# RWKV attention with a squared-ReLU feed-forward layer on one core: state products inside the mixing step, one pool of four PSUM banks, a re-calibrated planner with new order tables

## The chip, the cores and the metric

The kernel runs on one core of a Trainium2 chip, as one program. The metric is device time in microseconds, median of three runs. TensorE (PE) multiplies matrices into PSUM, of which the kernel uses eight banks of 128 partitions x 512 fp32; VectorE (DVE), ScalarE (ACT) and GpSimd (POOL) compute element-wise; SyncE (SP) issues nearly all transfers. Each engine works through its instructions in program order, and semaphores order the engines among each other.

## What is computed

```python
# r, k, v, w: (4, 8, 768, 48); u: (8, 48); w_in: (384, 2048); w_out: (2048, 384)
for t in range(S):
    kt, vt, rt, wt = (k[:, :, t], v[:, :, t], r[:, :, t], w[:, :, t])
    cur = np.einsum('bhd,bhe->bhde', u[None] * kt, vt)
    y[:, :, t] = np.einsum('bhd,bhde->bhe', rt, state + cur)
    state = wt[:, :, :, None] * state + np.einsum('bhd,bhe->bhde', kt, vt)
x = y.transpose(0, 2, 1, 3).reshape(B * S, H * D)
h = np.maximum(x @ w_in, 0.0)
return (h * h) @ w_out
```

The recurrence has 768 steps, four batches and eight heads of 48; its output is 3072 rows of 384 for the feed-forward layer.

## The kernel before

The sequence is cut into six chunks (c = 0 to 5) of 128 tokens. An attention unit is one chunk of one batch (24 units); heads lie in four pairs, each pair on 112 partitions. Inside a chunk the recurrence becomes matrix products: w is accumulated by a scan, and r and k are scaled by the products of w.

The steps of a unit, with their lines: transfers of w, k, r (L449 in chunk 0, L455 later) and v (L486); in chunk 0 three `turn` steps on TensorE (L502) that bring the inputs into the transposed layout by fp32 products with a permutation, later a DVE transpose (L464) and sixteen small transfers (L474); the scan (L514), logarithm and exponential (L521, L522), the scalings (L525, L548 to L551); `beta`, the sums for u (TensorE in chunk 0, L538; POOL and DVE later); the diagonal from beta (L561); the scores `mt` (L572, sixteen fp32 matmuls in the profile, into two banks); the causal mask (L576); `ktp` and `kt`, the transposed k (L584, L586); the mixing step `mix`, which adds state times r (`inter`, L604, 48-row weights) and scores times v (`part`, L612, 128-row weights); its split into a high and a low part (`x`, L644 and L645); and the state products `dS` (`outer`, L664, 128-row weights, v times k) that DVE and POOL add to the state (L670 to L673). A TensorE step of products on small fp32 tiles has a `mode` other than 0 in the plan; here "a visit" is a stretch of such steps with only other work (feed-forward products and transposes) before and after it.

The feed-forward layer runs over 16 column blocks f per chunk, for all four batches at once (128 x 512) or, in chunks 0 (f below 6) and 1, for two batches at a time (128 x 256): the first product `hp` (L693, nine matmuls), ReLU on ACT (L698), squaring on DVE or, in chunk 0, ACT (L702, L700), the split in a high and a low part (L704, L705), and the second product `ob` (L711, three matmuls for each batch). Weights come in eight groups (L396, L398; 1.57 MB a group) and are turned into a high and a low fp32r part (L409 to L430).

PSUM: four banks are the accumulators `ob`, two the pool `hp` of the first product, two the pool `a` of all attention steps. A score step or a mixing step from chunk 1 on needs two banks of `a` at once.

What sets the order: every step goes to `Plan.add` with an engine, an estimated cost, a rank, what it reads and writes, and the pool slots it needs. `Plan.order` simulates the engines with these costs and always takes the step that can start first, ties by rank; the steps are then emitted in that order, so the program's order is fixed when it is built. Ranks come from the tables in `Ranks` (L196 to L221). TensorE steps pay 0.094 us when the mode changes. Where the plan sees TensorE idle before 110 us it puts in transposes of the identity as fillers (L755), ten at the start. At the very end the overflow flag is made (L750 to L754) and read by all engines (L762).

## Time and profile before

| | |
|---|---|
| median of three runs | 545.43 us (544.31 to 545.88) |
| profiled execution, its own time | 546.6 us |
| its span, first to last instruction | 544.8 us |
| mean granted TensorE clock | 0.993 |
| TensorE busy | 532.6 us (98%), 4243 matmuls |
| VectorE, ScalarE, GpSimd busy | 351.4, 300.3, 94.5 us |
| first `turn` matmul, first feed-forward matmul | 5.77 us, 43.91 us |
| read from and written to HBM | 31.66 MB, 4.72 MB |

How to read it: times in the trace count from the first instruction. A row of the timeline gives start, length, engine, line, operation, output <- inputs, shapes and count; neighbouring matmuls of one line are merged, and the length runs to the end of the last, so the next row can start before it. Therefore costs are read from start to start. In a table by stretches each row has the stretch, its length, the busy time and count of PE, PEld (weight loads), DVE, ACT and POOL, then the granted TensorE clock, the share of the DMA engines and GB/s. A group row has the total busy time, the mean of one in ns, and the idle time before with what ended it. An fp32 matmul stands twice in the profile.

### The profile page before, as it was taken

How to read it: one execution, taken by the hardware profiler on the slowest of the kernel's cores; microseconds unless marked ns; L12 is line 12 of the kernel's file. 1: busy time of each engine (PE TensorE's matmuls, PEld its weight loads, DVE VectorE, ACT ScalarE, POOL GpSimd, SP SyncE). 2: the span in 40 equal slices, each digit the busy share in tenths (PEclk: the TensorE clock that was granted, in tenths of full speed). 3: DMA queues.
4: the chain of work that ended last, by engine and by line, in shares of the span. 5: the costliest groups of instructions: out<-in, count | busy, mean ns of one | idle time of the engine just before them, and what ended most of it. 6: DMA issues, size and time to landing. Idle time of an engine off the chain costs nothing.

```text
span 544.8 us, 11043 instructions
## 1 busy us (share of the span) xinstructions
PE 532.6 (98%) x4243; PEld 472.8 (87%) x4243; DVE 351.4 (65%) x653; ACT 300.3 (55%) x728; POOL 94.5 (17%) x111
## 2 busy tenths in 40 slices
PE   7999999999999999999999999999999999999994
PEld 7978998889998989888888888889888998999894
DVE  4899788989795959596685684948443333333331
ACT  2877989886756675583834377464332232333221
POOL 2046543634030301212030030200000000000000
PEclk9899999999999999999999999999999999999998
DMA  8998893665946576774668155770011000000001
GB/s 212 268 228 174 189 260 83 134 128 79 182 80 109 119 87 123 84 157 59 84 121 111 29 104 101 122 96 1 0 45 45 0 1 0 31 31 0 1 0 62
DMA packets 195913, 50.92 MB, mean 93 GB/s; under 512 B 184080, under 2 KB 190736, under 8 KB 195856
## 3 DMA queue, kind: packets, MB, share of 16 engines
q1 hardware_dynamic: 195536, 49.77, 47.3%
q8 instruction: 35, 0.57, 0.5%
q10 hardware_dynamic: 320, 0.40, 0.2%
q14 instruction: 22, 0.18, 0.1%
HBM read 31.66 MB, written 4.72 MB: 67 GB/s over the span
## 4 chain that ended last, share of the span: by engine, by line
PE 81%; SPq 6%; DMA 5%; DVE 5%; ACT 1%; issue 1%; DVEq 0%
PE hp L693 34%; PE ob L711 34%; SPq L474 4%; PE a L612 3%; DMA ri<-in_moe_w_in_dram 3%; PE a L572 3%; PE a L604 2%; PE a L664 2%; DMA pt<-st 1%; SPq L449 1%; DVE st L464 1%; PE a L584 1%; SPq L455 1%; SPq L486 1%; DVE pt L551 1%
## 5 line engine op out<-in xcount | busy, mean ns | idle before, releaser
L711 PE MATMUL ob<-wo,g 128*128 128x384 f32 x1152 | 227.0, 341 | 0.0
L693 PE MATMUL hp<-x,wi 128*128 128x512 f32 (+1 forms) x1062 | 222.7, 355 | 0.0
L711 PEld LDWEIGHTS ob<-wo,g 128*128 128x128 f32 x1152 | 200.1, 188 | 10.3 <-issue 2.6
L693 PEld LDWEIGHTS hp<-x,wi 128*128 128x128 f32 x1062 | 174.1, 188 | 26.2 <-issue 0.9
L698 ACT ACTIVATE t<-hp 128x512 f32<-128x512 f32 (+1 forms) x118 | 61.0, 517 | 120.6 <-PE hp L693 106.3
L702 DVE SCALAR_TENSOR_TENSOR hp<-hp,t 128x512 f32<-128x512 f32 (+1 forms) x96 | 58.2, 606 | 89.7 <-ACT t L698 89.3
L705 DVE TENSOR_TENSOR g<-hp,g 128x512 fp32r<-128x512 f32 (+1 forms) x118 | 69.0, 585 | 37.8 <-ACT g L704 37.0
L704 ACT CAST g<-hp 128x512 fp32r<-128x512 f32 (+1 forms) x118 | 59.6, 505 | 53.8 <-DVE hp L702 53.4
L561 ACT ACTIVATE m<-ident,beta 128x128 f32<-128x128 f32 x192 | 60.6, 398 | 1.2 <-DVE beta L546 1.1
L576 DVE COPY_PREDICATED m<-caus,a 128x512 f32<-128x512 uint8 x48 | 34.1, 733 | 6.4 <-PE a L572 5.0
L645 DVE SCALAR_TENSOR_TENSOR x<-a,x 112x128 fp32r<-112x128 f32 (+2 forms) x64 | 20.6, 345 | 24.1 <-ACT x L644 22.6
L514 DVE TENSOR_TENSOR_SCAN pt<-pt,zero 112x128 f32<-112x128 f32 x80 | 30.0, 422 | 5.7 <-DMA pt<-st 5.5
L644 ACT ACTIVATE x<-a 112x128 fp32r<-112x128 f32 (+2 forms) x64 | 18.5, 322 | 21.1 <-PE a L612 8.5
L572 PEld LDWEIGHTS a<-pt 48*128 48x128 f32 x384 | 23.9, 187 | 6.5 <-issue 3.2
L572 PE MATMUL a<-pt 48*128 48x128 f32 x384 | 28.7, 285 | 0.6 <-DVE pt L551 0.6
L612 PE MATMUL a<-m,v 128*48 128x128 f32 (+1 forms) x384 | 26.9, 279 | 0.4 <-DVE m L576 0.2
L543 POOL TENSOR_TENSOR st<-st 128x384 f32<-128x384 f32 x20 | 20.9, 1049 | 36.9 <-DVE st L464 27.9
L464 DVE STREAM_TRANSPOSE st<-st 128x1152 f32<-128x1152 f32 x20 | 26.4, 1352 | 0.5 <-DMA st<-in_r_dram 0.5
L530 POOL COPY Ec<-pt 112x4 f32<-112x4 f32 x20 | 7.4, 372 | 102.7 <-DVE pt L514 101.7
L612 PEld LDWEIGHTS a<-m,v 128*48 128x48 f32 (+1 forms) x384 | 19.9, 128 | 5.7 <-issue 4.2
L430 POOL TENSOR_TENSOR wi<-q,wi 128x768 fp32r<-128x768 f32 x8 | 16.8, 2100 | 29.4 <-ACT wi L429 23.1
L545 POOL TENSOR_TENSOR st<-st,un 128x384 f32<-128x384 f32 x20 | 21.4, 1072 | 1.3
(96 smaller groups left out, 432.9 us busy)
## 6 DMA issues: line engine op xcount, KB each, us to landing
pt<-st SPq DMA_DIRECT2D x80, 96.0 KB, 3.1
ro<-in_moe_w_out_dram SPq DMA_DIRECT2D x8, 768.0 KB, 6.8
v<-in_v_dram SPq DMA_DIRECT2D x24, 192.0 KB, 4.1
st<-in_w_dram SPq DMA_DIRECT2D x10, 384.0 KB, 3.7
st<-in_k_dram SPq DMA_DIRECT2D x10, 384.0 KB, 5.2
st<-in_r_dram SPq DMA_DIRECT2D x10, 384.0 KB, 5.3
pt<-st SPq DMA_DIRECT2D x80, 48.0 KB, 3.6
out_dram<-q SPq DMA_DIRECT2D x20, 192.0 KB, 2.5
```

What stands on the lines that cost most here:

```text
L464: V.transpose(out=zt[:, i].rearrange("a t p q i -> a t (p q) i"), in_=sv[:, :, i].rearrange("s t p q x -> s t (p q) x"))
L514: lambda p=p: V.tensor_tensor_scan(out=pt[:, 0, p], data0=src(0)[:, p], data1=zero.broadcast_to([HP, C]), initial=1.0, op0=ALU.mult, op1=A ...
L561: A.activation(mv(j)[:, p], ident, AF.Copy, scale=beta.tile[:, 2 * p + j:2 * p + j + 1])
L572: T.matmul(mts[j].tile.rearrange("s (p t) -> s p t", p=NP)[:, p], pt[js, 2, p], pt[js, 1, p], start=True, stop=True)
L576: lambda j=j: V.copy_predicated(out=mv(j), mask=caus.unsqueeze(1).broadcast_to([128, NP, C]), data=mts[j].tile.rearrange("s (p t) -> s p t ...
L612: T.matmul(spot(p)[to:to + n + D], vt.tile[:, o - n:o + D], mv(j)[:, p], start=(c == 0 and p == SPLIT), stop=True, skip_group_check=True)
L693: T.matmul(hp.tile[:, 0:n], wi[f][:, wl, kt], xT[:, kt, xl, xs], start=(m == 0), stop=(m == 3 * KT - 1))
L698: P.add("act", 0.5 if full else 0.28, rank("g"), lambda: A.activation(t(), h(), AF.Relu), r=[hp], w=[(g, 1)])
L702: P.add("dve", 0.61 if full else 0.33, rank("g"), lambda: V.scalar_tensor_tensor(out=h(), in0=h(), scalar=0.0, in1=t(), op0=ALU.max, op1=A ...
L704: P.add("act", 0.53 if full else 0.31, rank("g"), lambda: A.copy(out=hi(), in_=h()), r=[hp], w=[(g, 0)])
L705: P.add("dve", 0.61 if full else 0.33, rank("g"), lambda: V.tensor_tensor(out=lo(), in0=h(), in1=hi().bitcast(F32), op=ALU.subtract), r=[h ...
L711: T.matmul(obs[b][:, 0:DM], g.tile[0][:, gl, o:o + C], wo[f][:, wl], start=(f == 0 and m == 0), stop=(f == NF - 1 and m == 2))
```

## The change

- The state products move from a step of their own (`dS`) into the mixing step of chunks 1 to 4: `mix` now runs `outer`, `inter`, `part`. Their results lie in the free columns of the bank `far_yb`, so no further bank is taken. Chunk 0 keeps its `dS` step; chunk 5 has no state.
- `hp` and `a` become one pool of four banks, which the first feed-forward product shares with all attention steps.
- The planner: engines begin at given times, a transfer has its own issue cost, costs are adjusted, entering small tiles costs 0.095, leaving them 0.28, a change between two small shapes 0.1, and an engine may wait up to 0.02 to 0.055 us for a step of better rank. Before 7.8 us TensorE steps count 1.9 times. `KEEP`, which made small-tile steps stay together, becomes a large negative number.
- All order tables are new, and a table `F` moves single steps.
- The transposed u is made after the first `turn`, the flag's matmul gets an early rank, and the tile `gap` (16 columns) moves the addresses of what follows.

```diff
-    SWITCH, KEEP = 0.094, 1.0
+    BEGIN = {"sp": 0.8, "pe": 3.75, "dve": 3.0, "pool": 3.4, "act": 2.1}
+    ENTER, LEAVE, SWAP, KEEP = 0.095, 0.28, 0.1, -1189.25
+    HOLD = {"pe": 0.042, "act": 0.055, "dve": 0.0264}
+    COLD, filler, WARM = 7.8, None, 10
...
-                    if pick is None or (t, order) < (at, first_order):
-                        at, pick, first_order = t, s, order
+                    can.append((t, order, s))
+                if can:
+                    limit = min(x[0] for x in can) + self.HOLD.get(unit, 0.0)
+                    at, _, pick = min((x for x in can if x[0] <= limit), key=lambda x: x[1])
...
-                bank = next((x[1] for p in ("a", "hp") for x in self.pools.get(p, ()) if x[0] <= idle), None)
+                bank = next((x[1] for x in self.pools["a"] if x[0] <= idle), None)
...
-                        free[unit] += self.SWITCH
+                        free[unit] += self.SWAP if mode and s.mode else self.ENTER if s.mode else self.LEAVE
...
-    OFF = {'hp': 1, 'g': -172, 'ob': 6.25, 'os': -416.25}
+    OFF = {'hp': 1063.5, 'g': -7297.25, 'ob': 9685.5, 'os': 2989.25}
...
-    P.pool("hp", hps)
-    P.pool("a", pas)
+    P.pool("a", pas + hps)
...
+        dS = far_yb if c else Slot("a")
+        dv = lambda: dS.tile[0:HP, NP * C - NP * J:].rearrange("a (p e) -> a p e", p=NP)[:, :, 0:D]
...
             def mix():
+                if not last:
+                    outer()
                 inter()
                 part((*TILES, SPLIT))()
...
-            mixed = P.add("pe", 1.45, rank("mix"), mix, r=[vt, *Ms, ("S", b), *RK], w=[yb, far_yb], mode=3, claim=[x3])
+            P.add("pe", 1.44 if last else 1.88, rank("mix"), mix, r=[vt, *Ms, ("S", b), *RK, *(() if last else (Kt,))], w=[yb, far_yb], mode=3, claim=[x3])
...
-            P.add("pe", 0.5, rank("dS"), outer, r=[vt, Kt], w=[dS], mode=3, after=[mixed] if c else [])
+            if c == 0:
+                P.add("pe", 0.443, rank("dS"), outer, r=[vt, Kt], w=[dS], mode=3)
...
-        hp, g = Slot("hp"), Slot("g")
+        hp, g = Slot("a"), Slot("g")
```

What the order makes of it on TensorE around the state of one pair of batches, before (`a_148` and `a_149` are the attention banks, `ob` the accumulators, L664 the state products of two units, L711 and L693 feed-forward):

```order
L711 MATMUL ob_144<-wo_67,g_98 128x384 x3
L711 MATMUL ob_145<-wo_67,g_98 128x384 x3
L664 MATMUL a_148<-v_154,m_159 64x48
L664 MATMUL a_148<-v_154,m_159 48x48
...
L664 MATMUL a_149<-v_155,m_163 64x48
L664 MATMUL a_149<-v_155,m_163 48x48
...
L711 MATMUL ob_144<-wo_67,g_100 128x384 x3
L693 MATMUL hp_146<-x_134,wi_73 128x256 x9
```

and in the changed kernel around a pair of mixing steps (L660 the state products, L653 `inter`, L668 `part`, L618 scores, L743 the first feed-forward product):

```order
L618 MATMUL a_149<-pt_131 128x128
L660 MATMUL a_150<-v_156,m_162 64x48
...
L653 MATMUL hp_148<-pt_131,S_134 64x128
...
L668 MATMUL hp_148<-m_161,v_156 64x128
...
L660 MATMUL a_149<-v_157,m_164 64x48
...
L653 MATMUL hp_147<-pt_131,S_135 64x128
...
L668 MATMUL hp_147<-m_160,v_157 64x128
...
L743 MATMUL hp_148<-x_136,wi_65 128x256 x9
L743 MATMUL a_150<-x_136,wi_69 128x256 x9
```

The state products no longer stand between feed-forward steps; scores and two mixing steps follow one another, they take all four banks, and the first feed-forward products come straight behind them in the same banks. In the whole program the visits go from 61 to 41: from 49 to 28 in chunks 1 to 5, and from 12 to 13 in chunk 0.

The beginning of SP's queue before (`st` are inputs of chunk 0, `ri` and `ro` raw weights):

```order
L449 DMA st_136<-in_w_dram 128x1x384
L449 DMA st_136<-in_k_dram 128x1x384
L449 DMA st_136<-in_r_dram 128x1x384
...
L486 DMA v_91<-in_v_dram 128x8x48
L449 DMA st_137<-in_w_dram 128x1x384
...
L396 DMA ri_56<-in_moe_w_in_dram 112x512 x2
```

and now:

```order
L439 DMA ri_68<-in_moe_w_in_dram 112x512 x2
L439 DMA ri_68<-in_moe_w_in_dram 48x512 x2
L439 DMA ri_68<-in_moe_w_in_dram 16x2x512 x2
L441 DMA ro_70<-in_moe_w_out_dram 128x2x768
L492 DMA st_138<-in_w_dram 128x1x384
L492 DMA st_138<-in_k_dram 128x1x384
```

A whole weight group (group 3) now stands ahead of the first inputs of chunk 0.

The beginning of TensorE's queue before (L755 are fillers, L363 the transposed u):

```order
L755 MATMUL a_148<-ident 128x128 x10
L363 MATMUL hp_146<-ident,m_158 112x8
L502 MATMUL ob_142<-perm,st_136 64x64
L502 MATMUL ob_142<-perm,st_136 48x64
L502 MATMUL ob_142<-perm,st_136 64x64
```

and now:

```order
L805 MATMUL a_149<-ident 128x128 x58
L545 MATMUL ob_143<-perm,st_138 64x64
L545 MATMUL ob_143<-perm,st_138 48x64
L545 MATMUL ob_143<-perm,st_138 64x64
L545 MATMUL ob_143<-perm,st_138 48x64
```

There are 58 fillers ahead of the first turn, and none anywhere later; before there were ten, and 64 more between the steps of chunk 0.

More of the change, by code (lines that the diff above doesn't have):

```diff
@@ L55, in pool, with add @@
         self.pools[name] = [[0.0, t] for t in tiles]
-    def add(self, engine, cost, rank, fn, r=(), w=(), after=(), runs=128, port=False, mode=0, claim=()):
+    def add(self, engine, cost, rank, fn, r=(), w=(), after=(), runs=128, port=False, mode=0, claim=(), issue=0.64):
         s = Step()
@@ L361 @@
         nc.scalar.dma_start(out=u8[:, j * J:j * J + D], in_=u)
-    us = Slot("hp")
-    P.add("pe", 0.1, -300, lambda: T.transpose(out=us.tile[0:HP, 0:H], in_=u8, identity=ident[0:H, 0:H]), w=[us])
+    us = Slot("a")
     def columns():
@@ L395, in load_w @@
             n = 2 * PC if i > KT else to.shape[0]
-            P.add("sp", 0.4 if i > KT else 0.0059 * n, rank, lambda to=to, src=src: nc.sync.dma_start(out=to, in_=src),
-                  w=[("wi", g, i)], after=before, runs=n)
+            P.add("sp", 0.3 if i > KT else 0.0066 * n, rank, lambda to=to, src=src: nc.sync.dma_start(out=to, in_=src),
+                  w=[("wi", g, i)], after=before, runs=n, issue=0.46)
         P.add("sp", 2.4, rank, lambda: nc.sync.dma_start(out=wo_r[g], in_=w_out32[g]), w=[("wo", g, 0, 0)],
-              after=before, runs=256)
+              after=before, runs=256, issue=0.41)
     def split_w(g, rank):
@@ L502, in turn @@
                             T.matmul(to[j * J:j * J + n, :, :, y], rows[:, y * D:y * D + n], pick[:, :, j], start=True, stop=True, skip_group_check=True)
-                P.add("pe", 1.0, rank("turn"), turn, r=[(st, ui, i)], w=[ps[i]], mode=3)
+                turned = P.add("pe", 0.94, rank("turn"), turn, r=[(st, ui, i)], w=[ps[i]], mode=3)
+                if b == 0 and i == 0:
+                    P.add("pe", 0.1, rank("turn"), lambda: T.transpose(out=us.tile[0:HP, 0:H], in_=u8, identity=ident[0:H, 0:H]), w=[us], after=[turned])
+                    P.add("act", 0.3, rank("turn"), columns, r=[us], w=["ut"])
             def tl(x):
@@ L604, in inter, with outer @@
                     T.matmul(spot(p)[to:to + n + D], Ss[b][js, PC + p * D - n:PC + p * D + D], pt[js, 1, p],
[L605 removed]
+                             start=(p == 0 or p == 3 and last), stop=False, skip_group_check=True)
+        def outer():
+            for p in range(NP):
+                for j in range(2):
+                    o, n = vo(2 * p + j), (J, D)[j]
+                    T.matmul(dv()[j * J:j * J + n, p], kv(Kt)[:, p, j * J:j * J + n], vt.tile[:, o:o + D],
+                             start=(p == 0), stop=True, skip_group_check=True)
         def part(ps):
@@ L695, in ffn @@
         full = n == 512
-        P.add("pe", 2.09 if full else 1.07, rank("hp"), first, r=wkeys("wi") + [x for b in range(*bs) for x in xkeys(c, b)], w=[hp])
+        P.add("pe", 2.085 if full else 1.067, rank("hp"), first, r=wkeys("wi") + [x for b in range(*bs) for x in xkeys(c, b)], w=[hp])
         hi, lo, t, h = (lambda: g.tile[0][:, 0, 0:n]), (lambda: g.tile[0][:, 1, 0:n]), (lambda: g.tile[1][:, 0:n]), (lambda: hp.tile[:, 0:n])
```

97 lines of the change are left out of this document (47 added, 50 removed), and 33 rows, old and new, of the table F.

## The prediction

> **What bounds the kernel now.** I began with the page's head and its chain of waits.
>
> ```profile
> span 544.8 us, 11043 instructions
> ...
> PE 532.6 (98%) x4243; PEld 472.8 (87%) x4243; DVE 351.4 (65%) x653; ACT 300.3 (55%) x728; POOL 94.5 (17%) x111
> ...
> GB/s 212 268 228 174 189 260 83 134 128 79 182 80 109 119 87 123 84 157 59 84 121 111 29 104 101 122 96 1 0 45 45 0 1 0 31 31 0 1 0 62
> ...
> PE 81%; SPq 6%; DMA 5%; DVE 5%; ACT 1%; issue 1%; DVEq 0%
> ```
>
> TensorE is busy for 98% of the span and 81% of the chain. The profiled execution took 546.6 us for a span of 544.8, 1.2 above the median of 545.43 of the three timed runs. I work out a difference on the span and take it from that median. A measurement of this kernel can tell about 0.3% (1.6 us) from no change.
>
> Next, the table by stretches of time:
>
> ```profile
> 20.00:40.00 20.00, 19.71 (x280) 17.15 (x277) 18.97 (x33) 15.74 (x39) 5.47 (x5) 0.96 1.01 238
> 100.00:120.00 20.00, 20.00 (x176) 16.97 (x175) 17.34 (x29) 18.44 (x46) 9.44 (x9) 1.00 0.63 100
> 500.00:520.00 20.00, 20.00 (x102) 18.10 (x101) 6.59 (x10) 5.38 (x10) 0.00 (x0) 1.00 0.00 1
> ```
>
> The second number is TensorE: 20.00 of 20.00 in the later rows, and no other engine is as full. So after the first 45 us a change gains only by taking work, or the dead time between matmuls, from TensorE. In the first 45 us the transfers are full too (DMA share 1.01), and TensorE's busy time there contains fill-in transposes. So I priced two things apart: the visits to attention work in the steady part, and the start.
>
> **A visit and its price.** The timeline around three visits of the state products (L664), and an undisturbed stretch:
>
> ```profile
> 145.90 2.88 PE L711 MATMUL ob<-wo,g 128*128 128x384 f32 x15
> 148.70 0.67 PE L664 MATMUL a<-v,m 128*64 128x48 f32 x16
> 149.30 0.79 PE L711 MATMUL ob<-wo,g 128*128 128x384 f32 x3
> 149.93 1.23 PE L693 MATMUL hp<-x,wi 128*128 128x256 f32 x9
> 151.09 0.67 PE L664 MATMUL a<-v,m 128*64 128x48 f32 x16
> ...
> 234.07 1.13 PE L664 MATMUL a<-v,m 128*64 128x48 f32 x32
> 235.13 2.38 PE L693 MATMUL hp<-x,wi 128*128 128x512 f32 x9
> ...
> 447.13 2.27 PE L711 MATMUL ob<-wo,g 128*128 128x384 f32 x12
> 449.24 2.26 PE L693 MATMUL hp<-x,wi 128*128 128x512 f32 x9
> 451.34 2.27 PE L711 MATMUL ob<-wo,g 128*128 128x384 f32 x12
> ```
>
> I go from start to start. Undisturbed, twelve L711 take 2.11 (0.53 for three) and nine L693 of 512 columns 2.10 (1.05 for nine of 256). Sixteen L664 alone take 149.30 - 148.70 = 0.60; thirty-two in one visit take 1.06. So a step costs 0.46 in work and 0.14 to finish; the three L711 after it take 0.63 (0.10 more), the nine L693 ahead of the next visit 1.16 (0.11 more). One visit to small fp32 tiles costs 0.14 + 0.10 + 0.11 = 0.35 beyond its work.
>
> **The change, term by term.**
>
> *Visits.* The instruction order has 61 stretches of such work between other work before and 41 now: in chunks 1 to 5, 49 become 28 (nine were state products by themselves, the rest are score and mixing steps that now stand side by side), and chunk 0 has 13 for 12. 20 x 0.35 = -7.0 (bounds 0.33 to 0.38 each). The products themselves stay, 0.46 a step.
>
> *Changes of shape inside.* Each of 16 merged steps goes from 128-row products to 48-row ones, which a separate step did at its edge; four more score steps now stand directly against other attention work. The nearest rows:
>
> ```profile
> 311.93 0.67 PE L604 MATMUL a<-pt,S 48*64 48x128 f32 x16
> 312.53 1.09 PE L612 MATMUL a<-m,v 128*64 128x128 f32 x16
> ```
>
> Sixteen L604 up to the change to 128 rows take 0.60, where sixteen matmuls of the state step take 0.46: at most 0.14 for a change, at least 0. I take 0.1: 16 x 0.1 = +1.6 and 4 x 0.1 = +0.4. The Trainium skill speaks against the merger here: its page "TensorEngine Tiling (Array Packing)", section Key Properties, says that changing the tiling mode drains TensorE. By it the merger would keep the drain and only move it; the sum with the full price stands below as a rival.
>
> *A later start.* Now the rows of the start:
>
> ```profile
> 0.81 0.70 SPq L449 DMA_DIRECT2D st<-in_w_dram  x1
> ...
> st<-in_w_dram SPq DMA_DIRECT2D x4, 192.0 KB, 3.8
> ...
> 18.00:20.00 2.00, 2.00 (x44) 2.00 (x44) 1.37 (x3) 2.00 (x7) 0.00 (x0) 0.52 1.14 294
> ```
>
> ```profile
> 1.60 2.39 PE L755 MATMUL a<-ident 128*128 128x128 f32 x10 [1.60 <-POOL ident masks.py:199]
> ...
> 5.77 6.42 PE L502 MATMUL ob<-perm,st 128*64 128x64 f32 x128
> 12.12 1.05 PE L538 MATMUL ob<-ut,pt 112*128 112x2 f32 x8
> 13.11 2.08 PE L502 MATMUL hp<-perm,st 128*64 128x64 f32 x64
> ...
> 26.89 2.73 PE L755 MATMUL a<-ident 128*128 128x128 f32 x23
> 29.56 1.57 PE L572 MATMUL a<-pt 48*128 48x128 f32 x16
> 31.05 1.86 PE L755 MATMUL hp<-ident 128*128 128x128 f32 x15
> ...
> 43.91 2.26 PE L693 MATMUL hp<-x,wi 128*128 128x256 f32 x17
> ```
>
> SP's first seven issues now fetch weight group 3, 1.57 MB, ahead of the first attention input. At 212 GB/s (first slice of the page) to 294 (18 to 20 us) these take 5.3 to 7.4 us; with issue at 0.81 and 3.8 to land, the first turn starts at 9.9 to 12.0. TensorE meanwhile does 58 transposes from 1.60 on: at the first ten's rate (2.39 for ten) till 15.5, at the rate of 26.89 to 29.56 (2.67 for 23) till 8.3. With some twenty slow ones it is 1.6 + 20 x 0.24 + 38 x 0.116 = 10.8. I take 10.5, against 5.77: +4.7 (bounds +4.1 to +9.7).
>
> *Faster first turns.* 128 turn matmuls took 12.12 - 5.77 = 6.35, while 64 later took 1.87 (2.08 less the last one's 0.2), so 3.74 for 128: the first ran at half rate. After 58 transposes they should run at full rate: -2.6 (bound: 0).
>
> *Waits of chunk 0.* The fill-in transposes show how long TensorE waited there:
>
> ```profile
> L755 PE MATMUL a<-ident 128*128 128x128 f32 x46 | 6.8, 309 | 1.6 <-POOL ident masks.py:199 1.6
> L755 PE MATMUL hp<-ident 128*128 128x128 f32 x28 | 4.3, 281 | 0.0
> ```
>
> 6.8 + 4.3 less the first ten's 2.4 is 8.7 us of waiting. The new order has two score steps ahead of the first feed-forward product (43.91 here) instead of three, and takes batch 1 right through to its state before batch 0. The chains from scan to mask that TensorE waits for stay as long, and the pauses are no longer filled. I take -1.0: one score step's work of about 1 us moves out of the way. On SP the values (v) of batch 2 now stand behind 11.6 MB: five weight groups, twelve inputs and five other v. At 236 GB/s (mean of the page's first three slices) they land near 50 us, about when their mixing step is due; a TensorE wait of up to 3 us there is the upper bound. Bounds -4 and +3.
>
> *Tail.*
>
> ```profile
> 537.31 0.19 PE L753 MATMUL a<-one,flag 128*1 128x1 f32 x2
> 537.54 0.15 DVE L754 TENSOR_SCALAR flag_i<-a 1x1 int32<-1x1 f32 x1 [3.71 <-PE a L753]
> 537.61 0.91 DVE L719 COPY m<-ob 128x384 f32<-128x384 f32 x2
> ```
>
> The last copies stand behind the flag; it goes early now: -0.2.
>
> *Shared banks.* What empties a bank, of feed-forward (L698, L702) and of the mixing step (L645):
>
> ```profile
> L698 ACT ACTIVATE t<-hp 128x512 f32<-128x512 f32 (+1 forms) x118 | 61.0, 517 | 120.6 <-PE hp L693 106.3
> L702 DVE SCALAR_TENSOR_TENSOR hp<-hp,t 128x512 f32<-128x512 f32 (+1 forms) x96 | 58.2, 606 | 89.7 <-ACT t L698 89.3
> L645 DVE SCALAR_TENSOR_TENSOR x<-a,x 112x128 fp32r<-112x128 f32 (+2 forms) x64 | 20.6, 345 | 24.1 <-ACT x L644 22.6
> ```
>
> Before, feed-forward had two banks to itself; ACT then waited for TensorE 106.3 us in all, so those banks were ready in time. Now two mixing steps in a row hold all four, and a product behind them needs one emptied (about one L645 of 0.35 and its ACT partner). Much of this lies under the second mixing step or L711 work; where that cover is gone, 0.35 is a wait. TensorE runs in order, so a waiting first product holds back the second products (L711) queued behind it, which need no bank. I take +1.5, four or five such waits in 28 visits; bounds 0 and 28 x 0.35 = +9.8. DVE and ACT have no more work than before. The re-ordered transfers after chunk 0 lie beside TensorE work, at well under half of the rate that the first slices show; I cost them at nothing, and a late one would show as a TensorE gap.
>
> **Sum.** -7.0 + 1.6 + 0.4 + 4.7 - 2.6 - 1.0 - 0.2 + 1.5 = -2.6: span 542.2, median 542.8.
>
> **Rivals.**
> Better: chunk 0's waits shrink by 4 instead of 1, and the banks cost nothing: -2.6 - 3.0 - 1.5 = -7.1, 538.3. For it: with four banks, products can run ahead while attention waits. Against: the chains to the masks are as long as before. 0.22.
>
> The gain given back, by the clock. In the row of 18 to 20 us the granted clock is 0.52, although TensorE counts as busy; ahead of it stood a pause and the two-column products (L538), with hardly any streaming. The new order has unfilled pauses between such steps. One half-rate spell of some 3.4 us costs 1.7: one more than before gives 544.5, two 546.2. 0.18. The Trainium skill, "TensorE: Matmul & The Clock Gate", section "Why this matters for your kernels", asks only that gaps stay under about 3 us, by which nothing would be lost here; the row with 0.52 came without such a gap.
>
> The drain stays inside: a change of shape at the whole price of a visit, 16 x 0.35 = 5.6 in place of 1.6, gives -2.6 + 4.0 = +1.4, 546.8, still within 0.3%. Against: 0.60 for sixteen L604 leaves no room for 0.35. 0.08. This is what the tiling page's rule would make of it.
>
> Slower, by the banks: each of the 28 visits in chunks 1 to 5 makes a feed-forward product wait for a bank. At 0.35 each the sum is -2.6 - 1.5 + 9.8 = +5.7, 551.1; it becomes slower by more than 0.3% above (2.6 + 1.5 + 1.6) / 28 = 0.20 a visit. For it: pairs of mixing steps hold all four banks. Against: ACT and DVE have idle time everywhere after 100 us. 0.14.
>
> Slower, by cold transposes: they do not raise the clock; the fillers end at 15.5 and the turns stay at half rate: -2.6 + 5.0 + 2.6 = +5.0, 550.4. The row that bears on it:
>
> ```profile
> 28.40:31.80 3.40, 3.40 (x35) 3.00 (x34) 3.30 (x8) 3.40 (x11) 3.01 (x2) 1.00 1.12 216
> ```
>
> There more than half the time is transposes (26.89 to 29.56 and from 31.05), and the clock stays 1.00. 0.05. The same page of the Trainium skill, "Part 4: PE-mode transpose", says that transposes do not count as busy for the clock; the trace disagrees here.
>
> That the order is not what the change says can be left out: it is fixed when the program is built.
>
> **How the numbers follow.** The forecast has 0.33, the better case 0.22: faster 0.55. Spells of clock and the drain: within 0.3%, 0.26. Banks and cold transposes: slower, 0.19. The likeliest is 542.8. The range goes from 538.0 (the better case, a little under) to 548.5, which leaves out most of the two slow cases and little else.
>
> **What would show it.** Right: 41 visits; in the timeline no L664-like step by itself in chunks 1 to 5, a merged step of about 2.0 to 2.2 us; the first turn at about 10.5 and 128 turn matmuls in under 4 us; the first feed-forward product between 40 and 43. Wrong: TensorE gaps ahead of feed-forward products with ACT or DVE as releasers, adding to more than 5 us; a merged step over 2.3; granted clock under 0.7 in a stretch between 20 and 50 us; or a first turn after 13.

## The result and the profile after

| | before | changed |
|---|---|---|
| median of 20 runs, us | 545.43 (544.31 to 547.05) | 550.32 (545.20 to 554.68) |
| ratio to before | 1 | 1.0083, 95% interval 1.0062 to 1.0104 |
| profiled execution, us | 546.6 | 551.53 |
| its span, us, and mean granted clock | 544.8, 0.993 | 549.8, 0.980 |

The change makes the kernel slower by 0.8%; 542.8 had been forecast, and 550.32 lies above the range. The ratio leaves out the execution of 554.68, which is over 1.5% above the fastest. The changed kernel's times also spread more than before, and they go with the clock: 545.20 at a mean granted clock of 0.993, 553.30 at 0.981.

The head of the page after, with the row of the granted clock in 40 slices of 13.7 us:

```profile
span 549.8 us, 11008 instructions
...
PE 531.7 (97%) x4227; PEld 476.6 (87%) x4227; DVE 354.9 (65%) x653; ACT 299.4 (54%) x728; POOL 93.8 (17%) x111
...
PEclk9867999999999999999999999999999999999999
...
PE 82%; DMA 5%; ACT 4%; DVE 4%; SPq 2%; issue 1%; DVEq 0%; ACTq 0%
```

TensorE still bounds the kernel. What is new is the 8, 6 and 7 in the slices from 14 to 55 us. The table by stretches, cut at the places where the clock changes (after the engines' busy times: clock, DMA share, GB/s):

```profile
18.90:22.34 3.44, 3.17 (x52) 3.07 (x54) 3.04 (x4) 3.35 (x12) 1.83 (x1) 1.00 0.87 255
22.34:25.76 3.42, 3.42 (x66) 3.30 (x65) 3.07 (x8) 3.42 (x12) 0.17 (x1) 0.50 0.77 228
25.76:29.17 3.41, 1.89 (x22) 1.28 (x20) 2.53 (x5) 2.39 (x6) 1.43 (x2) 1.00 1.05 195
29.17:36.00 6.83, 6.83 (x69) 6.46 (x69) 4.57 (x7) 5.38 (x17) 2.34 (x1) 0.50 0.96 218
36.00:39.41 3.41, 2.30 (x38) 1.85 (x34) 2.48 (x7) 3.13 (x8) 0.67 (x2) 1.00 1.04 303
39.41:46.24 6.83, 6.69 (x67) 5.35 (x69) 4.58 (x8) 4.06 (x8) 1.50 (x2) 0.50 0.92 262
53.06:56.48 3.42, 3.42 (x19) 3.20 (x18) 3.14 (x6) 1.36 (x4) 0.00 (x0) 0.50 1.10 246
```

The 1.89 of 3.41 and 2.30 of 3.41 are stretches with pauses; the stretch behind each runs at half rate, and TensorE counts as busy in nearly all of it. Half rate lasts 3.42 + 6.83 + 6.83 + 3.42 = 20.5 us, where the kernel before has one spell of 3.4 (18.1 to 21.5). Now TensorE's timeline at the start (in brackets the idle time and its releaser):

```profile
1.61 8.32 PE L805 MATMUL a<-ident 128*128 128x128 f32 x58 [1.61 <-POOL ident masks.py:199]
10.83 3.86 PE L545 MATMUL ob<-perm,st 128*64 128x64 f32 x127 [0.91 <-DMA st<-in_w_dram]
14.51 0.22 PE L545 MATMUL a<-perm,st 128*48 128x64 f32 x1
14.53 0.22 PE L545 MATMUL ob<-perm,st 128*64 128x64 f32 x1
...
28.23 0.42 PE L668 MATMUL a<-m,v 128*48 128x128 f32 x2 [1.33 <-DVE m L622]
...
46.79 2.40 PE L743 MATMUL a<-x,wi 128*128 128x256 f32 x18
52.01 0.48 PE L618 MATMUL hp<-pt 48*128 48x128 f32 x2 [2.82 <-DVE pt L597]
```

The first turn starts at 10.83 and 128 turn matmuls take 14.53 - 10.83 = 3.70 (the 129th starts at 14.53), both as forecast. But the first feed-forward product comes at 46.79 instead of 40 to 43 (before: 43.91). And a merged step and a wait of the steady part:

```profile
176.08 0.60 PE L630 MATMUL hp<-ident,pt 112*128 112x112 f32 x4 [0.27 <-DVE g L755]
...
180.93 0.67 PE L660 MATMUL a<-v,m 128*64 128x48 f32 x16
181.53 0.32 PE L653 MATMUL hp<-pt,S 48*64 48x128 f32 x2
...
183.14 0.80 PE L761 MATMUL ob<-wo,g 128*128 128x384 f32 x3
```

The merged step takes 183.14 - 180.93 = 2.21. Of the 16 merged steps of the trace, six stand alone and take 2.21 each; ten stand in pairs, the first of a pair 2.11 and the second 2.17. L630 waits for a bank which VectorE's last feed-forward step (L755) still reads. In the groups of costs that is a new kind of idle time (last columns). The first row is of the kernel before, the others of the changed one:

```profile
L693 PE MATMUL hp<-x,wi 128*128 128x512 f32 (+1 forms) x1062 | 222.7, 355 | 0.0
...
L743 PE MATMUL hp<-x,wi 128*128 128x512 f32 (+1 forms) x513 | 106.8, 354 | 1.0 <-DVE g L755 1.0
...
L630 PE MATMUL a<-ident,pt 112*128 112x112 f32 x60 | 9.4, 284 | 0.3 <-DVE g L755 0.3
```

**Where the time is.** I priced every TensorE step by its undisturbed start-to-start time (first products 2.09 or 1.07, three second products 0.52, scores 0.92, mixing 1.44, merged 1.88, a visit 0.095 in and 0.283 out, a change between attention shapes 0.1) and took the sum off the time in the trace. What is left is waiting, half rate, and whatever a step takes beyond its price. The sums run to TensorE's last product:

| us | before | changed | changed, pauses filled (a_fill) |
|---|---|---|---|
| priced work and visits | 513.3 | 506.1 | 506.1 |
| left over, up to 60 us | 19.4 | 27.1 | 20.5 |
| left over, 60 to 402 us | 3.8 | 9.5 | 9.3 |
| left over, from 402 us on | 0.8 | -0.1 | 0.2 |

The visits bring what they should, 7.2 us: 20 fewer at 0.378 are 7.6, and 0.4 goes to the score steps that now stand against other attention work. The start takes 7.7 of it back and the stretch from 60 to 402 us another 5.7.

### The profile page after: what moved, and what is told of

It reads as the page before. It is cut to its first block, busy times and chain, and to the rows that moved or that the text cites. A ratio compares the mean times of both kernels' runs of the same rounds, so it can differ in the third digit from the quotient of the medians.

```text
span 549.8 us, 11008 instructions
## 1 busy us (share of the span) xinstructions
PE 531.7 (97%) x4227; PEld 476.6 (87%) x4227; DVE 354.9 (65%) x653; ACT 299.4 (54%) x728; POOL 93.8 (17%) x111
## 4 chain that ended last, share of the span: by engine, by line
PE 82%; DMA 5%; ACT 4%; DVE 4%; SPq 2%; issue 1%; DVEq 0%; ACTq 0%
PE ob L761 34%; PE a L743 17%; PE hp L743 16%; PE a L668 3%; PE a L618 3%; PE hp L618 2%; DMA ri<-in_moe_w_in_dram 2%; PE hp L668 2%; DMA st<-in_w_dram 1%; DMA st<-in_r_dram 1%; ACT m L607 1%; PE a L630 1%; DMA st<-in_k_dram 1%; PE a L653 1%; PE a L660 1%
## 5 line engine op out<-in xcount | busy, mean ns | idle before, releaser
L743 PE MATMUL a<-x,wi 128*128 128x512 f32 (+1 forms) x549 | 113.5, 355 | 0.0
L743 PE MATMUL hp<-x,wi 128*128 128x512 f32 (+1 forms) x513 | 106.8, 354 | 1.0 <-DVE g L755 1.0
L743 PEld LDWEIGHTS a<-x,wi 128*128 128x128 f32 x549 | 90.4, 191 | 15.1 <-DVE g L755 1.1
L743 PEld LDWEIGHTS hp<-x,wi 128*128 128x128 f32 x513 | 84.6, 189 | 15.1 <-DVE g L755 2.3
L748 ACT ACTIVATE t<-a 128x512 f32<-128x512 f32 (+1 forms) x61 | 31.5, 518 | 55.0 <-PE ob L761 49.3
L748 ACT ACTIVATE t<-hp 128x512 f32<-128x512 f32 (+1 forms) x57 | 29.6, 520 | 57.1 <-PE ob L761 55.8
L755 DVE TENSOR_TENSOR g<-a,g 128x512 fp32r<-128x512 f32 (+1 forms) x61 | 35.3, 583 | 19.3 <-ACT g L754 19.3
L755 DVE TENSOR_TENSOR g<-hp,g 128x512 fp32r<-128x512 f32 (+1 forms) x57 | 33.4, 586 | 20.6 <-ACT g L754 20.1
L754 ACT CAST g<-a 128x512 fp32r<-128x512 f32 (+1 forms) x61 | 30.5, 506 | 23.3 <-DVE a L752 23.1
L754 ACT CAST g<-hp 128x512 fp32r<-128x512 f32 (+1 forms) x57 | 28.9, 507 | 20.7 <-DVE hp L752 20.5
L589 POOL TENSOR_TENSOR st<-st 128x384 f32<-128x384 f32 x20 | 20.5, 1031 | 102.7 <-DVE st L507 93.3
L618 PE MATMUL hp<-pt 48*128 48x128 f32 x184 | 23.2, 285 | 2.8 <-DVE pt L597 2.8
L618 PE MATMUL a<-pt 48*128 48x128 f32 x200 | 24.8, 287 | 1.1 <-DVE x L703 0.6
L702 ACT ACTIVATE x<-a 112x128 fp32r<-112x128 f32 (+2 forms) x33 | 10.2, 325 | 27.1 <-PE a L668 24.2
L618 PEld LDWEIGHTS a<-pt 48*128 48x128 f32 x200 | 20.7, 188 | 4.3 <-issue 1.9
```

Of the source, the lines that this page charges most:

```text
L589: P.add("pool", 1.0, rank("rk"), lambda: G.tensor_tensor(out=rk(), in0=rk(), in1=vals(2), op=ALU.mult), r=[(st, ui, 2)], w=[(st, ui, 1)])
L618: T.matmul(mts[j].tile.rearrange("s (p t) -> s p t", p=NP)[:, p], pt[js, 2, p], pt[js, 1, p], start=True, stop=True)
L743: T.matmul(hp.tile[:, 0:n], wi[f][:, wl, kt], xT[:, kt, xl, xs], start=(m == 0), stop=(m == 3 * KT - 1))
L748: P.add("act", 0.5 if full else 0.28, rank("g"), lambda: A.activation(t(), h(), AF.Relu), r=[hp], w=[(g, 1)])
L754: P.add("act", 0.53 if full else 0.31, rank("g"), lambda: A.copy(out=hi(), in_=h()), r=[hp], w=[(g, 0)])
L755: P.add("dve", 0.61 if full else 0.33, rank("g"), lambda: V.tensor_tensor(out=lo(), in0=h(), in1=hi().bitcast(F32), op=ALU.subtract), r=[h ...
```

## The experiments

Each was timed against the kernel before on the same chip. In names, a is made from the changed kernel, b from the kernel before. The ratio is to before. The diffs show the lines that matter, with `...` for others; where a line begins with `lambda`, only the changed call of it is shown.

**a_fill: the pauses of chunk 0 filled.** Orders are unchanged; P.home is a corner of a bank that is free then.

```diff
+    MORE = {8: 6, 10: 2, 14: 16, 20: 8, 21: 14, 28: 18}
...
+            if s.engine == "pe":
+                for _ in range(self.MORE.get(pe, 0) if self.filler else 0):
+                    self.filler(self.home)
+                pe += 1
```

> The changed kernel, with 64 transposes of the identity added on TensorE ahead of the steps of chunk 0 that wait (6 before the beta products of unit 0, 2 before those of unit 1, 16 before unit 1's first mixing part, 8 and 14 before unit 0's scores and first mixing part, 18 before unit 2's scores); the planned order is the same. Theory A, the clock: the changed kernel ran 20.5 us of chunk 0 at a granted clock of 0.5 because those pauses stand empty; filled, at most two of the six half-rate windows of 3.4 us are left, the mean clock goes from 0.980 to 0.990 or more, and the time falls from 550.3 to 544.5 to 547.5. Theory B, the waits: the time goes into waits for banks and data, and the half rate only fills pauses that are there anyhow; the time stays within 549 to 552, whatever the clock does.

546.68 us, ratio 1.0037 (1.0017 to 1.0058), 3.6 less than the changed kernel's median. The stretches, the first feed-forward product and the fillers' group:

```profile
20.00:40.00 20.00, 20.00 (x334) 18.13 (x334) 18.88 (x32) 19.62 (x53) 8.01 (x6) 1.00 0.96 252
40.00:60.00 20.00, 18.48 (x185) 16.96 (x180) 19.89 (x29) 16.33 (x40) 8.19 (x5) 1.00 0.96 239
```

```profile
40.74 2.50 PE L749 MATMUL a<-x,wi 128*128 128x256 f32 x18
```

```profile
L811 PE MATMUL ob<-ident 128*128 128x128 f32 x64 | 8.2, 277 | 0.0
```

The clock stays at 1.00, and the first feed-forward product comes at 40.74, where the forecast had it. In this trace 6.6 of the 7.7 us are gone. The traced execution (544.87) is one of its quicker ones and that of the changed kernel (551.53) one of its slower ones, so the medians move only by 3.6, the ratios by 0.0046 (2.5 us). Theory A holds, theory B falls.

**b_nofill: the same in reverse.** The kernel before loses its 64 fillers.

```diff
-                if at < self.IDLE[0] and bank is not None:
+                if at < 15 and bank is not None:
```

> The kernel before without the 64 transposes of the identity that it issues in the pauses of chunk 0 (those ahead of the first turn stay out of it as they are; the order is the same). Theory A, the clock: the pauses then bring the half rate here too, three to six more windows of 3.4 us, the mean clock falls from 0.993 to about 0.98, and the time rises by 3 to 6 us, to 548.5 to 551.5. Theory B: the fillers only fill, and the time stays at 545 to 546, or falls by up to 0.3.

548.65 us, ratio 1.0055 (1.0037 to 1.0073): 3.8 slower in the median, 3.0 by the ratio, mean clock 0.981. Its stretch and two rows of TensorE's timeline:

```profile
20.00:40.00 20.00, 15.49 (x196) 13.10 (x192) 17.80 (x30) 14.53 (x36) 5.21 (x5) 0.67 1.05 246
```

```profile
30.11 1.16 PE L572 MATMUL a<-pt 48*128 48x128 f32 x14 [1.06 <-DVE pt L551]
32.81 2.68 PE L572 MATMUL a<-pt 48*128 48x128 f32 x16 [1.54 <-DVE m L576]
```

The kernel before had 0.96 in that row. The sixteen score matmuls of the last row took 1.61 there, and now 2.68. The first feed-forward product comes at 46.60 instead of 43.91. So a kernel with none of the change loses about as much as soon as its pauses stand empty.

**a_last: the state products last in the merged step.**

```diff
...
-                if not last:
-                    outer()
                 inter()
                 part((*TILES, SPLIT))()
+                if not last:
+                    outer()
```

Further lines move the flag that opens a bank to the product that now comes first in it.

> The changed kernel with one thing moved: in the 16 merged steps of chunks 1 to 4 the state products are issued last, behind the value products that have the same operand shape, instead of first, ahead of the products with the state. Theory C, the shape change: the merged step takes 2.21 us where its parts sum to 2.06, because the operand shape changes twice inside it; with one change it takes 2.05 to 2.10, and the time falls by 16 times 0.12 to 0.16, about 2 to 2.5 us, to 547.5 to 549. Theory D, the products themselves: the step stays at 2.18 to 2.24 in either order, and the time stays at 550. The clock of chunk 0 moves the whole time by up to 3 us either way, so the length of the step decides.

548.55 us, ratio 1.0070 (1.0048 to 1.0091). One merged step and the start of the next:

```profile
138.36 0.32 PE L653 MATMUL hp<-pt,S 48*64 48x128 f32 x2
...
139.88 0.62 PE L660 MATMUL a<-v,m 128*48 128x48 f32 x16
140.43 0.32 PE L653 MATMUL a<-pt,S 48*64 48x128 f32 x2
```

140.43 - 138.36 = 2.07. The 16 merged steps take 2.07 each, where in the changed kernel six took 2.21, five 2.11 and five 2.17: 6 x 0.14 + 5 x 0.04 + 5 x 0.10 = 1.5 us. Theory C holds for the step. The whole time falls by 1.8 in the median and 0.7 by the ratio; the intervals overlap.

**b_merge: the merge alone, two banks for attention as before.**

```diff
...
+        dS = far_yb if c else Slot("a")
...
             def mix():
+                if not last:
+                    outer()
                 inter()
...
-            P.add("pe", 0.5, rank("dS"), outer, r=[vt, Kt], w=[dS], mode=3, after=[mixed] if c else [])
+            if c == 0:
+                P.add("pe", 0.5, rank("dS"), outer, r=[vt, Kt], w=[dS], mode=3)
```

> The kernel before with the merge alone: in chunks 1 to 4 the state products stand inside the mixing step, in the second bank's free columns, issued first as in the changed kernel; pools, tables and planner stay. The plan then has 41 visits to the attention shapes in chunks 1 to 5 where it had 50. By the price of a visit, 0.35 to 0.38 us, that is 3.2 to 3.4 us less. Theory C, the shape change: 16 times 0.15 us are given back inside the merged steps, so the time falls by only 0.7 to 1.0, to about 544.6. Theory D, a step no longer than its parts: the time falls by 3, to about 542.3. Theory E, the banks: the second bank is now held until the state has been added, two banks are there, and the next unit's scores wait; the time is no lower than 545.4.

548.52 us, ratio 1.0063 (1.0039 to 1.0088): no gain, so neither C nor D; in the number it is E. But E's wait is not there: the scores (L572) wait 0.7 us in all. First products wait instead. Their group, the longest of these waits with what follows it, and VectorE ahead of it:

```profile
L697 PE MATMUL hp<-x,wi 128*128 128x512 f32 (+1 forms) x1062 | 223.1, 356 | 5.7 <-DVE g L709 5.7
```

```profile
178.89 1.42 PE L697 MATMUL hp<-x,wi 128*128 128x256 f32 x9 [2.60 <-DVE g L709]
180.11 2.12 PE L715 MATMUL ob<-wo,g 128*128 128x384 f32 x6
182.03 1.85 PE L697 MATMUL hp<-x,wi 128*128 128x256 f32 x9
```

```profile
175.18 0.74 DVE L514 TENSOR_TENSOR_SCAN pt<-pt,zero 112x128 f32<-112x128 f32 x2 [2.57 <-DMA v<-in_v_dram]
...
178.42 0.42 DVE L709 TENSOR_TENSOR g<-hp,g 128x256 fp32r<-128x256 f32 x1
```

VectorE's scan waits 2.57 us for a transfer, L709 stands behind it in the queue, and TensorE waits 2.60 for L709. The pause brings half rate here too: six L715 take 182.03 - 180.11 = 1.92 where 1.05 is usual. VectorE's state addition also waits longer:

```profile
L676 DVE TENSOR_TENSOR S<-a,S 112x192 f32<-112x192 f32 x16 | 5.7, 356 | 21.9 <-PE a L622 13.2 <-ACT x L656 8.5
```

The same addition in the kernel before:

```profile
L672 DVE TENSOR_TENSOR S<-a,S 112x192 f32<-112x192 f32 x16 | 5.5, 352 | 4.9 <-PE a L664 4.6
```

The state addition now comes out of the mixing step; VectorE waits for that step 13.2 us where it waited 4.6 for the step of its own. Whether that delays the transfers and the feed-forward steps, and so TensorE, is not shown. In this order the merge alone costs more than it brings.

**a_early: weight group 3 behind group 2.**

```diff
...
+        at = 1 + max(i for i, s in enumerate(order) if s.rank == RANKS.load(2))
+        order[at:at] = loads
+        at = min(i for i, s in enumerate(order) if s.rank == RANKS.split(4))
+        order[at:at] = splits
...
```

> The changed kernel with its seven loads of weight group 3 put behind those of group 2, and that group's split steps on ScalarE, VectorE and GpSimd ahead of group 4's, so that the first inputs are the first transfers; 30 transposes ahead of the first turn in place of 58. All other orders stay. Theory F, the late start: the first turn comes at 6.5 to 7.5 us instead of 10.8, the first feed-forward product 3 to 4 us earlier than at 46.8, and the time falls by 2 to 4 us, to 546.5 to 548.5. Theory G: what follows the turns is set by VectorE and by the clock of the unfilled pauses, which are then longer, so the first feed-forward product comes less than 1.5 us earlier and the time stays within 1.5 us of 550.

558.18 us, ratio 1.0229 (1.0205 to 1.0252). Both theories missed the time. The first turn comes at 7.35 and the first feed-forward product at 42.10, 4.7 earlier than in the changed kernel (F had 3 to 4), but then:

```profile
64.34 1.30 PE L772 MATMUL ob<-wo,g 128*128 128x384 f32 x6
72.88 1.09 PE L671 MATMUL hp<-v,m 128*64 128x48 f32 x16 [7.23 <-ACT m L643]
```

```profile
69.78 0.83 ACT L483 CAST wo<-q 128x768 fp32r<-128x768 f32 x1 [3.10 <-DVE q L476]
```

The edit puts the group's twelve split steps side by side; ScalarE's casts among them wait for VectorE, and the copy of the keys (L643) that TensorE needs stands behind them. So the run says nothing on what an earlier start brings in the end. **a_fill_last_early** is the same edit together with those of a_fill and a_last:

> The changed kernel with the 64 added transposes, the state products last in the merged step, and weight group 3 behind group 2, with 30 transposes ahead of the first turn. By theory F with A and C: 545.0 less 2 to 4, so 541 to 543, below the kernel before by 0.4 to 0.7%. By theory G: 544 to 546, as without the earlier start.

555.89 us, ratio 1.0184 (1.0146 to 1.0222), for the same reason.

**a_fill_last: both gains.** The edits of a_fill and a_last in one kernel.

> The changed kernel with both the 64 added transposes in the pauses of chunk 0 and the state products last in the merged step. By theories A and C the two gains are of different stages and add: 546.7 less 1.6 to 2.0, about 545.0. If the gain of the order inside the step came from the clock alone (0.980 to 0.988 there), it stays at 546.7.

546.10 us, ratio 1.0012 (0.9989 to 1.0035): 1.4 us less than a_fill by the ratio, 0.6 in the median, with overlapping intervals. In its trace the merged steps take 2.07, yet the time left over from 60 to 402 us is 9.5 where a_fill has 9.3: other waits stand in place of what the steps save.

**a_more_last: 110 fillers instead of 64.**

```diff
-    MORE = {8: 6, 10: 2, 14: 16, 20: 8, 21: 14, 28: 18}
+    MORE = {6: 6, 7: 6, 8: 8, 10: 4, 12: 4, 14: 18, 16: 4, 20: 10, 21: 16, 28: 32}
```

> The changed kernel with the state products last in the merged step and 110 added transposes in chunk 0 in place of 64 (32 instead of 18 before unit 2's scores, some before the turns of units 0 and 2 and before the beta products of units 1 and 2, a few more at each of the other places). Theory A: with 64, half-rate windows are still met in some executions, since the clock of their records goes from 0.990 to 0.998 and their times from 548.5 to 541.4; with the pauses fuller the clock is 0.996 or more in nearly all, and the median falls from 546.1 to 543 to 545, under the kernel before. Rival: the spread is of the transfers, not of the clock; then the median stays at 546, or rises by up to 1.5 for the fillers that stand where nothing waits.

547.46 us, ratio 1.0038 (1.0015 to 1.0061). Twelve executions at a clock of 0.994 to 0.999 still go from 545.62 to 550.22. So in the filled kernels the clock is no longer what spreads the times; what does is left open. The 46 further fillers bring no gain. In the median they cost 1.4 us, but the intervals overlap.

**a_fill_nofar: less work on ScalarE.** Made from a_fill; the range guard is not done in chunks 1 to 5.

```diff
-lambda: A.activation(vals(0), vals(0), AF.Square, bias=nmid)
+lambda: c or A.activation(vals(0), vals(0), AF.Square, bias=nmid)
...
-lambda: A.activation(vals(0), vals(0), AF.Relu, bias=nfar, accum_out=far[:, c * B + b:c * B + b + 1])
+lambda: A.copy(out=far[:, c * B + b:c * B + b + 1], in_=nmid) if c else A.activation(vals(0), vals(0), AF.Relu, bias=nfar, accum_out=far[:, c * B + b:c * B + b + 1])
```

> The changed kernel with the 64 added transposes, and with the range guard left out in chunks 1 to 5: its first ScalarE step is gone there and its second is a copy of one column, so 20 times about 1.1 us of ScalarE are not done; ranks, costs and orders are those of the changed kernel. Theory H, the releases: the feed-forward products of chunks 1 to 4 wait for banks and g buffers that ScalarE and VectorE release later than planned, 3 us more in the sum than before; with less on ScalarE the waits shrink and the time falls by 1 to 3 us, to 544 to 545.7. Theory I: the waits are VectorE's alone or those of PE's own order, and the time stays at 546.7 within 0.5.

545.40 us, ratio 1.0004 (0.9985 to 1.0022), 1.3 less than a_fill in the median, 1.8 by the ratio: at the low end of theory H, with intervals that overlap.

**a_bank: a shared bank released one VectorE step earlier.** Made from a_fill. The subtraction reads t instead of the bank, so the low part isn't the reference's.

```diff
-lambda: V.tensor_tensor(out=lo(), in0=h(), in1=hi().bitcast(F32), op=ALU.subtract)
+lambda: V.tensor_tensor(out=lo(), in0=t() if c > 0 else h(), in1=hi().bitcast(F32), op=ALU.subtract)
```

> The changed kernel with the 64 added transposes, and in chunks 1 to 5 the last feed-forward step on VectorE subtracts from the copy in SBUF instead of from the bank, so that the shared bank is released one VectorE step (about 0.6 us for a full product) earlier; what it computes there is not the reference's low part. All orders stay. Theory J, the shared banks: between 60 and 402 us the changed kernel's TensorE loses 9.3 us that are not priced work, the kernel before 3.8, and beside 1.8 for the shape changes that is 3.7 of waits for shared banks that VectorE's last step still reads; with the earlier release 2 to 3.5 of them go, and the time falls from 546.7 to 543.5 to 545. Theory K: they wait for g buffers, for masks and for state, and the time stays at 546.7 within 0.7.

544.08 us, ratio 0.9981 (0.9962 to 1.0000): 2.6 less than a_fill, as theory J has it. Yet in its traced execution the time left over from 60 to 402 us is 9.3 as in a_fill; of a_fill's five waits for that VectorE step, 1.6 us in all, one of 1.3 is left, and others (0.9 for masks, 1.0 for a transfer of v) have come. So the medians speak for theory J, and the trace does not show how.

**a_visits: 24 added visits in chunk 5.** Made from a_fill; EXTRA holds 24 second products.

```diff
...
+    P.visit = lambda: T.matmul(obs[0][0:48, 384:432], ident[0:48, 0:48], ident[0:48, 0:48], start=False, stop=False, skip_group_check=True)
...
+                if pe in self.EXTRA and self.filler:
+                    self.visit()
```

> The changed kernel with the 64 added transposes, and in chunk 5, between pairs of second products that stand side by side, 24 added visits to the attention shapes: one product of 48 by 48 elements each, into columns of a bank that nobody reads. Theory L, the price of a visit by the kernel before's rows: entering and leaving take 0.35 to 0.38 us and the product itself 0.02 to 0.06, so the 24 take 9 to 10.5 us, and the time rises from 546.7 to about 556.5. Rival: what is saved with a visit is only the time of its products and the pipeline hides the change of shape, so 24 visits take under 4 us, and the time stays below 551.

555.30 us, ratio 1.0186 (1.0159 to 1.0213), 8.6 more than a_fill. Two of the visits:

```profile
460.65 0.28 PE L816 MATMUL ob<-ident 48*48 48x48 f32 x2
460.87 1.31 PE L770 MATMUL ob<-wo,g 128*128 128x384 f32 x6
462.11 0.28 PE L816 MATMUL ob<-ident 48*48 48x48 f32 x2
```

462.11 - 460.65 = 1.46, less 1.05 for six second products, is 0.41 with the products themselves; 8.6 / 24 = 0.36. That is a little under theory L's 9 to 10.5 us and far from its rival's 4: the visit's price in the prediction, 0.35, was about right.

**a_sbuf: squares kept in SBUF, the bank free two steps earlier.** On top of a_fill_last; every step of the computation stays.

```diff
-lambda: A.activation(h(), t(), AF.Square)
+lambda: A.activation(t(), t(), AF.Square)
...
-lambda: V.scalar_tensor_tensor(out=h(), in0=h(), scalar=0.0, in1=t(), op0=ALU.max, op1=ALU.mult)
+lambda: V.scalar_tensor_tensor(out=t(), in0=h(), scalar=0.0, in1=t(), op0=ALU.max, op1=ALU.mult)
...
-lambda: A.copy(out=hi(), in_=h())
+lambda: A.copy(out=hi(), in_=t())
...
-lambda: V.tensor_tensor(out=lo(), in0=h(), in1=hi().bitcast(F32), op=ALU.subtract)
+lambda: V.tensor_tensor(out=lo(), in0=t(), in1=hi().bitcast(F32), op=ALU.subtract)
```

> The changed kernel with the 64 added transposes and the state products last in the merged step, and with the squared activations of the feed-forward kept in SBUF: the step on VectorE (in chunk 0 on ScalarE) that squares writes over the copy in SBUF and no longer back into the bank, and the two steps behind it read SBUF, so that a shared bank is free two steps earlier, about 1.2 us for a full product. Nothing is left out, and all orders of the main part stay. Theory J, the shared banks: the waits of the feed-forward products, scores and transposes of chunks 1 to 4 for a bank that VectorE's last step still reads go; the TensorE time that is not priced work falls from 9.3 to about 6 us between 60 and 402 us, and the time from 546.1 to 543 to 544.5, under the kernel before. Theory K: what they wait for is only partly a bank, and other waits (masks, transposed keys, g buffers) take the place of those that go, as one traced execution of the run with one step earlier showed; the sum between 60 and 402 us stays over 8, and the time at 545.5 or more.

544.10 us, ratio 0.9977 (0.9960 to 0.9995): 2.0 less than a_fill_last, 1.9 by the ratio, with intervals that just overlap. It is the one complete version below both kernels, and against the one before only by 0.2%. The group, and the wait that is longest now:

```profile
L749 PE MATMUL hp<-x,wi 128*128 128x512 f32 (+1 forms) x513 | 105.8, 352 | 0.4 <-DVE m L628 0.4
```

```profile
94.95 0.57 PE L636 MATMUL hp<-ident,pt 112*128 112x112 f32 x4 [0.84 <-ACT t L754]
```

The wait for VectorE's last step is gone from the first products. A bank that ScalarE still reads takes its place at 94.95, so the left-over time from 60 to 402 us only falls from 9.5 to 8.0: the time by theory J, the trace nearer to K.

**b_sbuf: the same edit in the kernel before.**

> The kernel before with the same edit: the squared activations stay in SBUF, and a bank is free two steps earlier. Its feed-forward has two banks of its own, and its products wait for nothing in the groups of costs. Theory J: the edit takes away waits for shared banks and there are none here, so the time stays within 0.5 us of 545. [...]

546.39 us, ratio 1.0022 (1.0004 to 1.0040): no gain, rather a loss, which theory J did not expect either. The steps that now read SBUF are slower: VectorE's subtraction takes 714 ns for a full product and 581 for a half one, where from the bank it took 686 and 415. So what pays in a_sbuf is the earlier release of the shared banks, not the edit by itself.

**a_sbuf_part: half of weight group 3 behind the first inputs.** Made from a_sbuf; `late` are the first three split steps of the output weights, `low` the fourth, and 34 transposes in place of 58 stand ahead of the first turn.

```diff
...
+        order.insert(next(i for i, s in enumerate(order) if s.rank == RANKS.unit(0, 1, "v")), load)
+        at = order.index(low)
+        order[at:at] = late
+        order[min(i for i, s in enumerate(order) if s.engine == "pe")].fill = 24, self.pools["a"][0][1]
```

> The kernel of the last experiment (added transposes, state products last, squares in SBUF) with half of weight group 3's transfers later: its output weights (one load of 768 KB) stand behind the six loads of units 0 and 1 in place of ahead of them, their first three split steps stand right ahead of the fourth, and 34 transposes instead of 58 precede the first turn. The other half of the group, and every queue behind unit 1's loads, keep their place. Theory F, the late start: the first turn comes 2.5 to 3.5 us earlier than in that kernel, the first feed-forward product 1.5 to 3 us, and the time falls from 544.1 to 541.5 to 543. Theory G: chunk 0 is bound by VectorE's chains and by the weight transfers, which run at 220 to 290 GB/s for 60 us whatever stands first; the first turn is earlier, but the time stays within 1 us of 544.1.

547.78 us, ratio 1.0039 (1.0011 to 1.0066), 3.7 more than a_sbuf. Two turns and a stretch:

```profile
7.62 3.89 PE L563 MATMUL ob<-perm,st 128*64 128x64 f32 x127
...
17.50 1.97 PE L563 MATMUL hp<-perm,st 128*64 128x64 f32 x32 [2.31 <-DMA st<-in_k_dram]
```

```profile
20.00:40.00 20.00, 20.00 (x264) 18.72 (x262) 14.15 (x27) 14.69 (x42) 6.12 (x5) 0.75 0.97 255
```

a_sbuf's first turns and first feed-forward product:

```profile
12.36 5.47 PE L551 MATMUL ob<-perm,st 128*64 128x64 f32 x128 [1.99 <-DMA st<-in_w_dram]
...
42.31 2.50 PE L749 MATMUL a<-x,wi 128*128 128x256 f32 x18
```

The first turn is 4.7 us earlier, then turns wait for the next inputs, and half rate follows from 16.3 to 29.9 us. The first feed-forward product comes 3.2 us later, at 45.55. Both theories missed: F expected a gain, G a time within 1 us. An earlier first turn gained nothing here, but what it would bring at full clock stays open, since the new pauses (2.31 at 17.50) have no fillers.

The shared pool by itself in the kernel before, separate banks in the changed kernel, and the planner's new costs and tables by themselves were not tried.

## Why the prediction was wrong

The terms as predicted, and as the two traces give them (changed against before, up to TensorE's last product; the spans differ by 5.0, the medians by 4.9):

| term, us | predicted | measured |
|---|---|---|
| visits, with 0.4 for the four score steps | -6.6 | -7.2 |
| shape changes in the 16 merged steps | +1.6 | +2.6 |
| later start | +4.7 | +5.1 |
| faster first turns | -2.6 | -2.6 |
| waits of chunk 0 (the rest of the 7.7 up to 60 us) | -1.0 | +5.2 |
| tail (from 402 us on) | -0.2 | -0.9 |
| shared banks (the rest of the 5.7 from 60 to 402 us) | +1.5 | +3.1 |
| sum | -2.6 | +5.3 |

The step that failed is **waits of chunk 0**. "The chains from scan to mask that TensorE waits for stay as long, and the pauses are no longer filled. I take -1.0": the working saw the empty pauses and gave them no price in the sum. In the two traces the term came to +5.2. It left the pauses to the rival of the clock, and that rival had the right mechanism and too small a size: one or two spells of 3.4 us more, where the trace shows 20.5 us at half rate against 3.4 before (the four rows at 0.50), so five more. The prediction's own sign for it, a clock under 0.7 between 20 and 50 us, came. As I read it, the loss feeds itself: at half rate the steps behind a pause take longer, VectorE's inputs come later, and the next window is thin again; that part is argued, not shown. What the clock costs is shown in both directions by a_fill and b_nofill, 2.5 and 3.0 us by the ratios, 3.6 and 3.8 in the medians.

Rows that were there pointed to it. Of the fillers' 11.1 us before, 8.7 stood in pauses, and the row of 28.40 to 31.80, more than half fillers, held 1.00. With those gone, that stretch too had to be counted as one that may fall.

**Visits** were right, and a_visits gives the price by itself. **Start** and **first turns** were right as times of the first turn. Whether a start moved by so much moves the end by as much is not shown: in a_sbuf_part an earlier one only waits at the next inputs, at half rate. The two terms and the waits behind them are better taken as one, over the whole stretch up to 60 us.

**Shape changes**: the price of a merged step is 1.44 + 0.44, and 0.175 for leaving where other work follows (a mixing step of the kernel before, priced 1.44, takes 0.60 + 1.02 to the next start). 2.21 is 0.155 above it in the six that stand alone, 2.17 is 0.11 above it in the five that end a pair, and 2.11 is 0.23 above 1.88 in the five that begin one: 2.6 in all, 0.16 a step. That is a little over the prediction's upper bound of 0.14 for a change. a_last takes 1.5 of it off the steps.

**Shared banks**: 5.7 left over from 60 to 402 us, less 2.6, is 3.1 for the predicted 1.5. This is a remainder; the profile names 1.6 of it as waits for VectorE's last feed-forward step. a_bank and a_sbuf give back 2.6 and 2.0 in the medians, 3.1 and 1.9 by the ratios. That an earlier release is worth this is shown; which single waits add to it is not, since in the traces others take their place.

The rival of the drain (546.8) is met in part only: a change of shape cost 0.16 a merged step, nearer to the 0.1 of the sum than to the 0.35 of a whole visit. Cold transposes (550.4) did not happen, since the turns ran at full rate. That 550.4 and the bank rival's 551.1 lie near the measured time is chance; the bank rival needed 0.20 us at each of 28 visits, and 3.1 / 28 is 0.11. The transfers ahead of batch 2's values add up to 5 x 1.57 + 17 x 0.197 = 11.2 MB, not 11.6; TensorE has no wait for them before 60 us.

## What to carry to other kernels

A pause of TensorE had two prices here: its length, and what the clock took from the work behind it. So when an edit removes fillers or moves waits, size the second from the profile's clock row in a stretch that had fillers, and put it in the sum. Fillers paid here where TensorE waited anyway. And buffers that two stages come to share are best freed early: writing a result to SBUF instead of back into the bank brought 2.0 us here.

## What the runs showed of the hardware

The granted clock changes between 1.00 and 0.50 alone. In the changed kernel a spell at 0.50 lasts 3.4 us or twice that; in b_nofill one lasts 10.2 (31.98 to 42.21), in a_sbuf_part 13.6 (16.30 to 29.94), three and four times 3.4. The clock falls without a long gap: ahead of the spell at 22.34 TensorE counted as busy for 3.17 us of 3.44 (18.90 to 22.34), with two-column products and short pauses, and ahead of the next one its longest wait was 1.33. The Trainium skill, "TensorE: Matmul & The Clock Gate", section "Why this matters for your kernels", asks for gaps under about 3 us; here that was not enough. The same page's section "A second HAM failure mode: psum-queue depth-cycling" says that many small idle times between groups of matmuls make the clock swing, and the rows from 22 to 57 us agree.

The profile's clock does not show the start. In the kernel before it reads 1.00 from 0 to 18 us, yet the first 128 turn matmuls took 6.35 there; in the changed kernel 17 transposes run in the 3.6 us from 1.60 on and 33 in the 3.4 us from 5.20 on, both at 1.00. So the mean clock leaves this part out.

Transposes of the identity raise the clock: 58 of them from 1.61 on, and the first turn runs at full rate, 3.70 us for 128 matmuls where the kernel before took 6.35. In a_fill, with 64 more in the pauses, the clock stays at 1.00 from 6 to 538 us. They do not hold it through a longer wait behind them: in a_sbuf the same 58 stand first, the first turn then waits 1.99 us for its inputs, the clock is 0.50 from 13.0 to 16.4, and 128 turn matmuls take 17.61 - 12.36 = 5.25.
